# One transformer block with two token streams on one core: scale and value weights loaded in other chunks, the value products ordered by key tile, and the text's normalisation moved ahead

## The chip, the cores and the metric

The kernel runs on one core of a Trainium2 chip. The metric is the device time of one execution in microseconds; of several runs the median is given. Everything below that is called the span is the stretch from the first to the last instruction that the profiler recorded.

## What is computed

There are two streams of tokens: 2 batches of 256 image tokens and 2 batches of 32 text tokens, each token with D = 1152 features. All inputs and outputs are bf16.

```python
mod_i = (_silu(c) @ wmod_img).reshape(B, 6, 1, D)      # the same for the text: mod_t
shi, sci, gai = mod_i[:, 0], mod_i[:, 1], mod_i[:, 2]  # shift, scale, gate
hi = _layernorm(x_img) * (1 + sci) + shi
ht = _layernorm(x_txt) * (1 + sct) + sht
qkvi = hi @ wqkv_img
qkvt = ht @ wqkv_txt
...                                                    # q, k, v: text tokens first, then image tokens
p = _softmax(jnp.einsum('bqd,bkd->bqk', q, k) * D ** (-0.5))
a = jnp.einsum('bqk,bkd->bqd', p, v)
out_i = x_img + gai * (ai @ wo_img)
out_t = x_txt + gat * (at @ wo_txt)
```

Of the modulation weights only three of the six column blocks (shift, scale, gate) are read, so the weights come to 14 blocks of 1152 x 1152, 2592 KB each.

## The kernel before

The 1152 features are nine tiles of 128 ("key tiles", `kt`), the 512 image tokens four tiles of 128 (`i` = 0 to 3, two for each batch). The order of the instructions on each engine is the order of the calls in the source: nothing reorders them. All weights come through SyncE's DMA queue in the order in which `dma_start` is called, into a pool of six 2592 KB buffers (`wpool`).

The first stage prepares the image tokens and makes the values. For each token tile, VectorE takes the statistics (`stats_of`, L153), ScalarE the standard deviation (`std_of`, L160) and VectorE the normalised tile `xn_i` (`out_of`, L164 and L165). TensorE transposes the nine 128 x 128 blocks of it (`x_transposes`, L178). ScalarE copies them out of PSUM into `hT_i`: `evac_scaled` (L183) multiplies by the scale while it copies, `evac_low` (L187) and `evac_high` (L190) copy without it. The transposes go to two PSUM tiles: `n0` blocks into the first, from the seven-slot pool `ps_mm`, and the rest into a second one, from `ps_mm` for token tiles 0 and 1, from the one-slot pool `ps_sm` for tiles 2 and 3 (`n0` = 8).

The scale itself, one column for each key tile, is 9 matmuls of two columns each for a key tile (`mod_scale`, L195), whose result is evicted with 1 added (L204 or L206). Where `hT_i` was copied out before its scale was known, `apply_mod` multiplies it in place, on VectorE (L214), GpSimd (L219) or ScalarE (L223).

The image values are the products of `hT_i` with `w_v_i`: for each token tile two halves of 512 columns (and a rest of 128, `v_rest`, L340), each a sum over nine key tiles in a PSUM tile of its own (`vacc`). `v_part` issues the matmuls of one such unit for one chunk of key tiles (L235), `v_block` loops over chunks and, inside, over units. Seven of the eight units are made here and sit in `ps_mm` until their ninth matmul; the seventh unit, token tile 3's first half, gets its slot when the last transposes have been copied out. `KC` cuts both weights into chunks of key tiles, (0,2), (2,4), (4,6) and (6,9): `load_sc` loads a chunk's columns of the scale weights (rows of 256 or 384 elements, 512 or 768 bytes), `load_v` a chunk's rows of the value weights (2304 bytes each). The queue's order is x0, x1, scale 0, x2, value 0, x3, then scale and value of chunks 1, 2 and 3, then the shift weights `w_sh_i` and the query weights `w_q_i`. `warm` issues matmuls on zeros (L130): 4, 7 and, behind `mod_scale(0)`, 3.

Then come the shift of the image tokens (rows of `strip_rows`, L361 and L365, columns by `select_cols`, additions by `apply_mod`) and the query stage, `qk_img(w_q_i, 0)`: nine groups of nine matmuls of 512 columns (L450), the first three groups together, each evicted by ScalarE or VectorE in turn (L434, L436). After it TensorE makes the rows of the text's shift (`tsh`), of its scale (`tsc`) and of the values' shift term (`svr`) by `rows_for_cols` (L361, L365), evicted on VectorE, ScalarE, VectorE (`evac`, L144 and L146). Then comes the key stage, `qk_img(w_k_i, 1)`, with three hooks between its groups: before group 0 `txt_norm` normalises the text (VectorE and ScalarE, L476 to L479, with a load of ScalarE's exponential table), before group 3 `all_cols` makes the scale and shift columns, and before group 6 `txt_transposes` transposes the normalised text on TensorE (L492) and modulates it on VectorE (L494, L496). Text queries and keys (L507), scores, softmax, attention and the output products follow.

Of the kernel before, what the change touches and what calls it, by code (L numbers as in the profile page):

```python
# [8 lines left out]
ACT = mybir.ActivationFunctionType  # L9
# [5 lines left out]
def kernel(  # L15
# [21 lines left out]
    P = 128  # L37
# [8 lines left out]
    SCALE = float(D) ** -0.5  # L46
    EPS = 1e-5

    KC = [(0, 2), (2, 4), (4, 6), (6, KT)]
    VW = 512  # L50
    NM = 1024

# [36 lines left out]
    def load_x(i):  # L89
        nc.sync.dma_start(x_i[:, i, :], xi_t[:, i, :])  # L90

    def load_sc(ch):
        k0, k1 = KC[ch]
        nc.sync.dma_start(w_sc_i[:, :, k0 * P:k1 * P], w_view(wmod_img)[:, :, D + k0 * P:D + k1 * P])  # L94

    def load_v(ch):
        k0, k1 = KC[ch]
        nc.sync.dma_start(w_v_i[:, k0:k1, :], w_view(wqkv_img)[:, k0:k1, 2 * D:3 * D])  # L98

    load_x(0)  # L100
    load_x(1)
    load_sc(0)
    load_x(2)
    load_v(0)
    load_x(3)
    for ch in range(1, len(KC)):
        load_sc(ch)
        load_v(ch)
    K3 = ((0, 3), (3, 6), (6, KT))
    K2 = ((0, 5), (5, KT))  # L110
    w_sh_i = load_w(wmod_img, 0)
# [15 lines left out]
    def warm(n):  # L127
        for _ in range(n):
            ps = ps_mm.tile([P, VW], f32, tag="mm", name="wps")
            nc.tensor.matmul(ps[:], lhsT=wz[:, 0:P], rhs=wz[:], start=True, stop=True)  # L130
# [41 lines left out]
    def x_transposes(i, n0=5):  # L172
        tps = (ps_mm.tile([P, n0, P], bf, tag="mm", name="tp"),
               ps_mm.tile([P, KT - n0, P], bf, tag="mm", name="tp") if n0 == 5 else
               ps_sm.tile([P, KT - n0, P], bf, tag="sm", name="tp"))
        for kt in range(KT):
            tp = tps[0][:, kt, :] if kt < n0 else tps[1][:, kt - n0, :]
            nc.tensor.transpose(tp, xn_i[:, i, kt * P:(kt + 1) * P], ident[:])  # L178
        return tps + (n0,)

    def evac_scaled(i, tps, n):
        for kt in range(n):
            nc.scalar.activation(hT_i[:, kt, i * P:(i + 1) * P], tps[0][:, kt, :], ACT.Identity,  # L183
                                 scale=mod_i[:, KT + kt, i // TPB:i // TPB + 1])

    def evac_low(i, tps, n):
        nc.scalar.copy(hT_i[:, n:tps[2], i * P:(i + 1) * P], tps[0][:, n:tps[2], :])  # L187

    def evac_high(i, tps):
        nc.scalar.copy(hT_i[:, tps[2]:KT, i * P:(i + 1) * P], tps[1][:])  # L190
# [7 lines left out]
    def mod_scale(ch, eng, own=True):  # L198
        k0, k1 = KC[ch]
        pool, tag = (ps_sm, "sm") if own else (ps_mm, "mm")  # L200
        mps = pool.tile([P, KT, B], f32, tag=tag)
        mod_cols(w_sc_i, mps, k0, k1)
        if eng == "dve":
            nc.vector.tensor_scalar_add(mod_i[:, KT + k0:KT + k1, :], mps[:, 0:k1 - k0, :], 1.0)  # L204
        else:
            nc.scalar.activation(mod_i[:, KT + k0:KT + k1, :], mps[:, 0:k1 - k0, :], ACT.Identity, bias=1.0)  # L206

    def apply_mod(kt, t0, t1, shift, eng):
        b = t0 // TPB
        sl = hT_i[:, kt, t0 * P:t1 * P]  # L210
        ap = mod_i[:, kt, b:b + 1] if shift else mod_i[:, KT + kt, b:b + 1]
        op = ALU.add if shift else ALU.mult
        if eng == 0:
            nc.vector.tensor_scalar(sl, sl, ap, None, op0=op)  # L214
        elif eng == 1:
            if shift:
                nc.gpsimd.tensor_scalar(sl, sl, 1.0, ap, op0=ALU.mult, op1=ALU.add)
            else:
                nc.gpsimd.tensor_scalar(sl, sl, ap, 0.0, op0=ALU.mult, op1=ALU.add)  # L219
        elif shift:  # L220
            nc.scalar.activation(sl, sl, ACT.Identity, bias=ap, scale=1.0)
        else:
            nc.scalar.activation(sl, sl, ACT.Identity, scale=ap)  # L223
# [2 lines left out]

    vacc = {}

    def v_part(i, half, ch):
        k0, k1 = KC[ch]  # L230
        if ch == 0:
            vacc[i, half] = ps_mm.tile([P, VW], f32, tag="mm", name=f"va{i}{half}")
        ps = vacc[i, half]
        for kt in range(k0, k1):
            nc.tensor.matmul(ps[:], lhsT=hT_i[:, kt, i * P:(i + 1) * P], rhs=w_v_i[:, kt, half * VW:(half + 1) * VW],  # L235
                             start=(kt == 0), stop=(kt == KT - 1))
        if k1 == KT:
            evac(v_i[:, i, half * VW:(half + 1) * VW], ps[:])


    def v_block(units, chs):
        for ch in chs:
            for (i, half) in units:
                v_part(i, half, ch)

    warm(4)
    silu_c()
# [3 lines left out]
    def stats_of(i, k0, k1):  # L251
        lns[i] = ln_stats(x_i[:, i, :], P, k0, k1, lns.get(i))

    def std_of(i):
        lns[i] = ln_std(lns[i], P)

    def out_of(i):
        ln_apply(x_i[:, i, :], P, xn_i[:, i, :], *lns[i])

    stats_of(0, 0, NCH)  # L260
    std_of(0)
    stats_of(1, 0, 1)
    out_of(0)
    tps = x_transposes(0)
    stats_of(1, 1, NCH)
    evac_low(0, tps, 2)
    std_of(1)
    mod_scale(0, "act")
    evac_scaled(0, tps, 2)
    evac_high(0, tps)  # L270
    out_of(1)
    warm(3)
    tps = x_transposes(1)
    stats_of(2, 0, NCH)
    evac_scaled(1, tps, 2)
    std_of(2)
    evac_low(1, tps, 2)
    evac_high(1, tps)
    stats_of(3, 0, 1)
    out_of(2)  # L280
    v_block([(0, 0), (0, 1), (1, 0), (1, 1)], [0])
    tps = x_transposes(2, KT - 1)
    stats_of(3, 1, NCH)
    evac_scaled(2, tps, 2)
    std_of(3)
    mod_scale(1, "dve", own=False)
    for n, kt in enumerate(range(*KC[1])):
        apply_mod(kt, 0, 2, False, n)
    evac_low(2, tps, 2)
    evac_high(2, tps)  # L290
    v_block([(2, 0), (2, 1)], [0])
    out_of(3)
    for kt in range(*KC[1]):
        apply_mod(kt, 2, 3, False, 0)
    v_block([(0, 0), (0, 1)], [1])
    tps = x_transposes(3, KT - 1)
    evac_high(3, tps)
    evac_scaled(3, tps, 4)
    evac_low(3, tps, 4)
    v_block([(1, 0), (1, 1)], [1])  # L300
    mod_scale(2, "dve")
    for kt in range(*KC[2]):
        apply_mod(kt, 0, 2, False, 0)
        apply_mod(kt, 2, 4, False, 1)
    v_block([(2, 0), (2, 1)], [1])
    v_block([(3, 0)], [0, 1])
    v_i = act.tile([P, NIT, D], bf, tag="A")
    SEVEN = [(i, half) for i in range(NIT) for half in range(2)][:7]
    for (i, half) in SEVEN[:4]:
        v_part(i, half, 2)  # L310
    mod_scale(3, "dve")
    for b in range(B):
        for n, kt in enumerate(range(*KC[3])):
            apply_mod(kt, b * TPB, (b + 1) * TPB, False, (n + b) % 3)
    for (i, half) in SEVEN[4:]:
        v_part(i, half, 2)
    for (i, half) in SEVEN:
        v_part(i, half, 3)

    selF = const.tile([P, 2, 2, B, NT], bf)
    for r in range(2):
# [76 lines left out]
    evac(v_i[:, 3, VW:NM], ps[:])  # L400
    nc.gpsimd.tensor_copy(shT32[:, :, 0:B], mod_i[:, 0:KT, :])

    w_sh_t = load_w(wmod_txt, 0, K2)
    w_sc_t = load_w(wmod_txt, D, K2)
    w_k_i = load_w(wqkv_img, D, K3)
    nc.sync.dma_start(x_t[:], xt_flat[:, :])
    w_q_t = load_w(wqkv_txt, 0)
    w_k_t = load_w(wqkv_txt, D)
    w_ga_i = load_w(wmod_img, 2 * D)
# [44 lines left out]

    qk_img(w_q_i, 0, hooks={})

    tsh = rows_for_cols(w_sh_t, "tsh")
    tsc = rows_for_cols(w_sc_t, "tsc")
    svr = rows_for_cols(w_v_i, "svr", lhs=shT32)
# [10 lines left out]
    mod_t = const.tile([P, 2, KT, B], f32, name="mod_txt")  # L470
    sv_full = const.tile([P, 2 * KT + 16 + 128], f32, name="sv")
    sv = sv_full[:, 0:KT * B].rearrange("p (k b) -> p k b", b=B)
    hT_t = act.tile([P, KT, NTT], bf)
    xn_t = act.tile([NTT, D], bf)

    def txt_norm():  # L476
        ln_apply(x_t[:, :], NTT, xn_t[:, :], *ln_std(ln_stats(x_t[:, :], NTT), NTT))
        junk = small.tile([P, 1], f32, bufs=1)
        nc.scalar.activation(junk[:], eps_t[:], ACT.Exp)  # L479

    def all_cols():
        ctp = ps_sm.tile([P, 3, NCOL + B], f32, tag="sm")
# [3 lines left out]
            cols_out(mod_t[:, k, :, :], ctp[:, k, :], float(k))  # L486
        cols_out(sv, ctp[:, 2, :], 0.0)

    def txt_transposes():
        tpt = ps_mm.tile([P, KT, NTT], bf, tag="mm")  # L490
        for kt in range(KT):
            nc.tensor.transpose(tpt[:, kt, :], xn_t[:, kt * P:(kt + 1) * P], ident[0:NTT, 0:NTT])  # L492
        hv = hT_t[:].rearrange("p k (b t) -> p k b t", b=B)
        nc.vector.tensor_mul(hv, tpt[:].rearrange("p k (b t) -> p k b t", b=B),  # L494
                             mod_t[:, 1, :, :].unsqueeze(3).to_broadcast([P, KT, B, NT]))
        nc.vector.tensor_add(hv, hv, mod_t[:, 0, :, :].unsqueeze(3).to_broadcast([P, KT, B, NT]))  # L496

    qk_img(w_k_i, 1, hooks={0: txt_norm, 3: all_cols, 6: txt_transposes})

    FG = 6  # L500
    for blk, wq in enumerate([w_q_t, w_k_t]):
# [341 lines left out]
```

## Time and profile before

| what | value |
|---|---|
| time, median of three runs (lowest, highest) | 117.24 us (117.14, 117.29) |
| time of the profiled execution | 117.79 us |
| its span | 115.8 us |
| TensorE busy in the span | 110.6 us, 96% |
| VectorE, ScalarE, GpSimd busy | 53.7, 34.2, 24.0 us |
| bytes read from HBM | 39.36 MB |
| DMA rate over the span | 351 GB/s |
| 162 matmuls of the query and key stages (L450) | 35.6 us busy |
| 63 matmuls of the value units (L235) | 14.6 us busy |

The page cuts the span into 40 slices of 2.9 us. TensorE is busy for nine tenths or more of each slice from the fifth to the last but one, and the 16 DMA engines from the second to the thirty-fifth:

```profile
PE   5978999999999999999999999999999999999990
...
DMA  3999999999999999999999999999999999982052
```

Each digit is the busy share of one slice in tenths. Most of the kernel is thus limited by TensorE while the weights stream in beside it; in the first slices TensorE works on what has arrived. The profiled execution took 0.55 us more than the median of the runs; its instruction times are used below as they are, and what they sum to is laid on the median.

### The profile page before, as it was taken

The page shows a single profiled execution, that of the slowest core. Times are in us where ns is not written, and L with a number is a line of the kernel's source. Part 1 is how long each engine was busy: PE and PEld are TensorE (multiplying, and loading weights), DVE is VectorE, ACT ScalarE, POOL GpSimd, SP SyncE. Part 2 cuts the span into 40 slices and gives each one's busy share as a digit, 9 for nine tenths or more (in the row PEclk, how much of TensorE's full clock was granted, in tenths as well). Part 3 has the DMA queues.
Part 4 walks back from the last instruction along what each step waited for, and adds up shares of the span by engine and source line. Part 5 has one row for each costly group of instructions (what it writes and reads, how often), then busy time and mean ns, then how long its engine had stood idle before and what let it go on. Part 6 is the DMA issues. An engine that isn't in the chain of part 4 may idle for free.

```text
span 115.8 us, 2947 instructions
## 1 busy us (share of the span) xinstructions
PE 110.6 (96%) x1262; PEld 65.3 (56%) x1262; DVE 53.7 (46%) x138; ACT 34.2 (30%) x83; POOL 24.0 (21%) x55
## 2 busy tenths in 40 slices
PE   5978999999999999999999999999999999999990
PEld 1344563548644444486444445987677665568570
DVE  1689920354290312211572332136665804994771
ACT  4548660343270320121080121116455700000200
POOL 4000103660050000002215000000240300999000
PEclk9999999999999999999999999999999999999999
DMA  3999999999999999999999999999999999982052
GB/s 83 297 338 359 376 385 399 409 412 415 404 408 408 413 412 400 414 410 294 375 404 411 396 376 381 404 412 402 412 408 405 404 416 410 409 297 108 6 187 68
DMA packets 22840, 40.89 MB, mean 353 GB/s; under 512 B 1183, under 2 KB 6699, under 8 KB 22827
## 3 DMA queue, kind: packets, MB, share of 16 engines
q1 hardware_dynamic: 22032, 39.82, 91.8%
q0 software_dynamic: 480, 0.73, 1.7%
q8 instruction: 10, 0.16, 0.5%
q10 hardware_dynamic: 315, 0.14, 0.5%
q14 instruction: 3, 0.02, 0.1%
HBM read 39.36 MB, written 1.34 MB: 351 GB/s over the span
## 4 chain that ended last, share of the span: by engine, by line
PE 80%; SPq 9%; DMA 8%; issue 1%; DVE 1%
PE qkps L450 30%; PE ps L762 15%; DMA w_sc_i<-in_wmod_img_dram 8%; PE va L235 5%; SPq L98 5%; PE aps L671 5%; PE ps L507 4%; PE sps L531 4%; PE gps L361 4%; SPq L90 3%; PE ops L783 2%; PE ps L395 2%; PE ps L340 2%; PE ps L603 2%; SPq L94 1%; PE gps L423 1%
## 5 line engine op out<-in xcount | busy, mean ns | idle before, releaser
L450 PE MATMUL qkps<-hT_i,t 128*128 128x512 bf16 x162 | 35.6, 379 | 0.0
L450 PEld LDWEIGHTS <-t 128*128 128x128 bf16 x162 | 15.6, 98 | 18.6
L762 PE MATMUL ps<-t,aT 128*128 128x384 bf16 x99 | 16.4, 326 | 0.0
L762 PEld LDWEIGHTS <-aT 128*128 128x128 bf16 x117 | 11.1, 98 | 6.7 <-issue 0.2
L235 PE MATMUL va<-w_v_i,hT_i 128*128 128x512 bf16 x63 | 14.6, 379 | 0.2 <-ACT hT_i L183 0.2
L746 POOL TENSOR_TENSOR w_og<-t,gb 128x384 bf16<-128x384 bf16 x9 | 8.7, 996 | 6.1 <-DMA gb<-mod_scratch 6.1
L235 PEld LDWEIGHTS <-hT_i 128*128 128x128 bf16 x63 | 5.8, 97 | 6.8 <-ACT hT_i L190 0.3
L768 DVE TENSOR_TENSOR tmp<-ps,gb 128x384 bf16<-128x384 f32 x11 | 6.0, 549 | 4.9 <-DMA gb<-mod_scratch 4.2
L434 DVE TENSOR_SCALAR qkT<-qkps 128x512 bf16<-128x512 f32 x4 | 2.8, 692 | 11.4 <-PE qkps L450 11.4
L153 DVE BATCH_NORM_STATS2 stats<-x_i 128x6 f32<-128x384 bf16 x12 | 6.0, 542 | 2.6 <-DMA x_i<-in_x_img_dram 2.6
L130 PE MATMUL wps<-wz 128*128 128x512 bf16 x14 | 5.9, 574 | 1.2 <-DVE wz L120 1.2
L436 ACT ACTIVATE qkT<-qkps 128x512 bf16<-128x512 f32 x5 | 2.9, 596 | 13.6 <-PE qkps L450 13.6
L144 DVE CAST qkT<-qkps 128x512 bf16<-128x512 f32 x4 | 2.8, 692 | 6.7 <-PE qkps L450 6.7
L219 POOL TENSOR_SCALAR hT_i<-hT_i,mod_img 128x256 bf16<-128x256 bf16 x5 | 2.5, 510 | 16.1 <-ACT rstd L160 9.6
L146 ACT CAST qkT<-qkps 128x512 bf16<-128x512 f32 x5 | 2.8, 582 | 9.7 <-PE qkps L450 9.7
L558 POOL DMA_DIRECT2D mod_scratch<-g_sb x2 | 1.2, 583 | 20.7 <-ACT g_sb L556 20.7
L769 DVE TENSOR_TENSOR o<-tmp,x_i 128x384 bf16<-128x384 bf16 x11 | 5.2, 471 | 0.4
L684 DVE TENSOR_SCALAR aT<-aps,sv 128x288 bf16<-128x288 f32 (+2 forms) x11 | 4.3, 456 | 2.3 <-PE aps L671 2.3
L507 PEld LDWEIGHTS <-t 128*128 128x128 bf16 x162 | 4.9, 98 | 0.2
L507 PE MATMUL ps<-hT_t,t 128*128 128x64 bf16 x162 | 4.9, 193 | 0.0
L738 ACT CAST gbf_full<-bps 128x288 bf16<-128x288 f32 x2 | 0.7, 402 | 14.2 <-PE bps L736 14.2
L671 PE MATMUL aps<-pT,v_i 128*128 128x288 bf16 (+2 forms) x44 | 4.8, 264 | 0.1
(156 smaller groups left out, 139.8 us busy)
## 6 DMA issues: line engine op xcount, KB each, us to landing
t<-in_wmod_img_dram SPq DMA_DIRECT2D x2, 2592.0 KB, 19.3
t<-in_wqkv_img_dram SPq DMA_DIRECT2D x6, 864.0 KB, 13.8
t<-in_wqkv_txt_dram SPq DMA_DIRECT2D x2, 2592.0 KB, 18.4
t<-in_wmod_txt_dram SPq DMA_DIRECT2D x2, 1440.0 KB, 15.0
t<-in_wqkv_txt_dram SPq DMA_DIRECT2D x3, 864.0 KB, 16.0
t<-in_wmod_txt_dram SPq DMA_DIRECT2D x1, 2592.0 KB, 19.5
t<-in_wo_txt_dram SPq DMA_DIRECT2D x3, 864.0 KB, 15.3
t<-in_wmod_txt_dram SPq DMA_DIRECT2D x2, 1152.0 KB, 16.2
```

Source lines behind the costliest of these rows:

```text
L98: nc.sync.dma_start(w_v_i[:, k0:k1, :], w_view(wqkv_img)[:, k0:k1, 2 * D:3 * D])
L130: nc.tensor.matmul(ps[:], lhsT=wz[:, 0:P], rhs=wz[:], start=True, stop=True)
L153: nc.vector.bn_stats(stats[0:np_, k, :], x_ap[:, k * CH:(k + 1) * CH])
L235: nc.tensor.matmul(ps[:], lhsT=hT_i[:, kt, i * P:(i + 1) * P], rhs=w_v_i[:, kt, half * VW:(half + 1) * VW], start=(kt == 0), stop=(kt == K ...
L361: nc.tensor.matmul(gps[32 * g:32 * g + 32, 0:RC], lhsT=lhs[:, kt, :], rhs=wt[:, kt, g * RC:(g + 1) * RC], start=(kt == 0), stop=(kt == KT ...
L450: nc.tensor.matmul(pss[j - j0][:], lhsT=wq[:, kt, j * P:(j + 1) * P], rhs=hT_i[:, kt, :], start=(kt == 0), stop=(kt == KT - 1))
L507: nc.tensor.matmul(ps[:, j - j0, :], lhsT=wq[:, kt, j * P:(j + 1) * P], rhs=hT_t[:, kt, :], start=(kt == 0), stop=(kt == KT - 1))
L671: nc.tensor.matmul(bank[:, off:off + c1 - c0], lhsT=lhsT, rhs=rhs, start=(first[id(bank)] == n), stop=(final[id(bank)] == n))
L746: nc.gpsimd.tensor_mul(w_og[:, dt, 0:CH], w_o_i[:, dt, NG0:D], gb[:, B - 1, NG0:D])
L762: nc.tensor.matmul(ps[:, 0:cw], lhsT=aT[:, dt, t0:t0 + P], rhs=rhs, start=(dt == DTS[0]), stop=(dt == DTS[-1]))
L768: nc.vector.tensor_mul(tmp[:, 0:cw], ps[:, 0:cw], gb[:, b, cs])
L769: nc.vector.tensor_add(o[:, cs], tmp[:, 0:cw], x_i[:, i, cs])
```

## The change

`KC` has three chunks of three key tiles in place of four. The scale weights come in three DMAs of 864 KB with rows of 768 bytes; the value weights come in single key tiles (288 KB) and pairs (576 KB): the queue's order is x0, x1, scale 0, x2, v0, v1, x3, v2, scale 1, v3, v4-5, scale 2, v6, v7-8. `v_k` replaces `v_part` and `v_block`: for each key tile, in the outer loop, one matmul of each unit. The order of the calls in the first stage is written anew around it. `warm(2)` stands ahead of `mod_scale(0)` in place of `warm(3)` behind it; `evac_high(0)` stands ahead of it too. The text's weights `w_sh_t` and `w_sc_t` are one DMA each and `x_t` is loaded ahead of `w_k_i`. The text is normalised behind the query stage, ahead of the rows `tsh`; it is transposed behind the rows `svr` and copied to `hT_t` by ScalarE, and VectorE modulates it in place at the key stage's group 6.

```diff
-    KC = [(0, 2), (2, 4), (4, 6), (6, KT)]
+    KC = [(0, 3), (3, 6), (6, KT)]
...
-    def load_v(ch):
-        k0, k1 = KC[ch]
+    def load_v(k0, k1):
         nc.sync.dma_start(w_v_i[:, k0:k1, :], w_view(wqkv_img)[:, k0:k1, 2 * D:3 * D])
...
     load_sc(0)
     load_x(2)
-    load_v(0)
+    load_v(0, 1)
+    load_v(1, 2)
     load_x(3)
+    load_v(2, 3)
     for ch in range(1, len(KC)):
+        k0, k1 = KC[ch]
         load_sc(ch)
-        load_v(ch)
+        load_v(k0, k0 + 1)
+        load_v(k0 + 1, k1)
...
-    def evac_scaled(i, tps, n):
-        for kt in range(n):
+    def evac_scaled(i, tps, n, n0=0):
+        for kt in range(n0, n):
...
-    def v_part(i, half, ch):
...
-    def v_block(units, chs):
...
+    def v_k(units, *kts):
+        for kt in kts:
             for (i, half) in units:
-                v_part(i, half, ch)
+                if kt == 0:
+                    vacc[i, half] = ps_mm.tile([P, VW], f32, tag="mm", name=f"va{i}{half}")
+                ps = vacc[i, half]
+                nc.tensor.matmul(ps[:], lhsT=hT_i[:, kt, i * P:(i + 1) * P], rhs=w_v_i[:, kt, half * VW:(half + 1) * VW],
+                                 start=(kt == 0), stop=(kt == KT - 1))
+                if kt == KT - 1:
+                    evac(v_i[:, i, half * VW:(half + 1) * VW], ps[:])
...
+    U = [[(i, half) for half in range(2)] for i in range(NIT - 1)] + [[(NIT - 1, 0)]]
+    U01, U012, UALL = U[0] + U[1], U[0] + U[1] + U[2], U[0] + U[1] + U[2] + U[3]
...
     tps = x_transposes(0)
+    evac_low(0, tps, 3)
+    warm(2)
     stats_of(1, 1, NCH)
-    evac_low(0, tps, 2)
     std_of(1)
+    evac_high(0, tps)
     mod_scale(0, "act")
-    evac_scaled(0, tps, 2)
-    evac_high(0, tps)
+    evac_scaled(0, tps, 3)
     out_of(1)
-    warm(3)
     tps = x_transposes(1)
     stats_of(2, 0, NCH)
     evac_scaled(1, tps, 2)
     std_of(2)
-    evac_low(1, tps, 2)
+    evac_scaled(1, tps, 3, 2)
+    evac_low(1, tps, 3)
     evac_high(1, tps)
-    stats_of(3, 0, 1)
     out_of(2)
-    v_block([(0, 0), (0, 1), (1, 0), (1, 1)], [0])
+    v_k(U01, 0, 1)
     tps = x_transposes(2, KT - 1)
-    stats_of(3, 1, NCH)
-    evac_scaled(2, tps, 2)
+    stats_of(3, 0, NCH)
+    evac_scaled(2, tps, 3)
     std_of(3)
-    mod_scale(1, "dve", own=False)
-    for n, kt in enumerate(range(*KC[1])):
-        apply_mod(kt, 0, 2, False, n)
-    evac_low(2, tps, 2)
+    evac_low(2, tps, 3)
     evac_high(2, tps)
-    v_block([(2, 0), (2, 1)], [0])
     out_of(3)
+    v_k(U01, 2)
+    v_k(U[2], 0, 1, 2)
+    mod_scale(1, "dve")
     for kt in range(*KC[1]):
-        apply_mod(kt, 2, 3, False, 0)
-    v_block([(0, 0), (0, 1)], [1])
+        apply_mod(kt, 0, 2, False, 0)
+        apply_mod(kt, 2, 3, False, 1)
     tps = x_transposes(3, KT - 1)
+    evac_scaled(3, tps, 3)
+    evac_low(3, tps, 3)
     evac_high(3, tps)
-    evac_scaled(3, tps, 4)
-    evac_low(3, tps, 4)
-    v_block([(1, 0), (1, 1)], [1])
+    for kt in range(*KC[1]):
+        apply_mod(kt, 3, 4, False, 0)
+    v_k(U012, 3)
+    v_k(U[3], 0, 1, 2)
+    v_i = act.tile([P, NIT, D], bf, tag="A")
+    v_k(U012, 4)
+    v_k(U[3], 3, 4)
     mod_scale(2, "dve")
...
+    v_k(UALL, *range(5, KT))
...
-    w_sh_t = load_w(wmod_txt, 0, K2)
-    w_sc_t = load_w(wmod_txt, D, K2)
+    w_sh_t = load_w(wmod_txt, 0)
+    w_sc_t = load_w(wmod_txt, D)
+    nc.sync.dma_start(x_t[:], xt_flat[:, :])
     w_k_i = load_w(wqkv_img, D, K3)
-    nc.sync.dma_start(x_t[:], xt_flat[:, :])
...
     qk_img(w_q_i, 0, hooks={})
 
+    hT_t = act.tile([P, KT, NTT], bf)
+    xn_t = act.tile([NTT, D], bf)
+    ln_apply(x_t[:, :], NTT, xn_t[:, :], *ln_std(ln_stats(x_t[:, :], NTT), NTT))
+    junk = small.tile([P, 1], f32, bufs=1)
+    nc.scalar.activation(junk[:], eps_t[:], ACT.Exp)
     tsh = rows_for_cols(w_sh_t, "tsh")
     tsc = rows_for_cols(w_sc_t, "tsc")
     svr = rows_for_cols(w_v_i, "svr", lhs=shT32)
...
+    tpt = ps_mm.tile([P, KT, NTT], bf, tag="mm")
+    for kt in range(KT):
+        nc.tensor.transpose(tpt[:, kt, :], xn_t[:, kt * P:(kt + 1) * P], ident[0:NTT, 0:NTT])
+    nc.scalar.copy(hT_t[:], tpt[:])
...
-    def txt_transposes():
...
+    def txt_mod():
         hv = hT_t[:].rearrange("p k (b t) -> p k b t", b=B)
-        nc.vector.tensor_mul(hv, tpt[:].rearrange("p k (b t) -> p k b t", b=B),
-                             mod_t[:, 1, :, :].unsqueeze(3).to_broadcast([P, KT, B, NT]))
+        nc.vector.tensor_mul(hv, hv, mod_t[:, 1, :, :].unsqueeze(3).to_broadcast([P, KT, B, NT]))
         nc.vector.tensor_add(hv, hv, mod_t[:, 0, :, :].unsqueeze(3).to_broadcast([P, KT, B, NT]))
 
-    qk_img(w_k_i, 1, hooks={0: txt_norm, 3: all_cols, 6: txt_transposes})
+    qk_img(w_k_i, 1, hooks={3: all_cols, 6: txt_mod})
```

More of the change, by code (lines that the diff above doesn't have):

```diff
@@ L227 @@
     vacc = {}
-    def v_part(i, half, ch):
[L230 to L238, printed above, removed]
-    def v_block(units, chs):
-        for ch in chs:
-            for (i, half) in units:
-                v_part(i, half, ch)
+    def v_k(units, *kts):
+        for kt in kts:
+            for (i, half) in units:
+                if kt == 0:
[5 more added lines that the diff above has]
+                    evac(v_i[:, i, half * VW:(half + 1) * VW], ps[:])
     warm(4)
@@ L276 @@
     std_of(2)
-    evac_low(1, tps, 2)
+    evac_scaled(1, tps, 3, 2)
+    evac_low(1, tps, 3)
     evac_high(1, tps)
-    stats_of(3, 0, 1)
     out_of(2)
-    v_block([(0, 0), (0, 1), (1, 0), (1, 1)], [0])
+    v_k(U01, 0, 1)
     tps = x_transposes(2, KT - 1)
-    stats_of(3, 1, NCH)
-    evac_scaled(2, tps, 2)
+    stats_of(3, 0, NCH)
+    evac_scaled(2, tps, 3)
     std_of(3)
-    mod_scale(1, "dve", own=False)
-    for n, kt in enumerate(range(*KC[1])):
-        apply_mod(kt, 0, 2, False, n)
-    evac_low(2, tps, 2)
+    evac_low(2, tps, 3)
     evac_high(2, tps)
-    v_block([(2, 0), (2, 1)], [0])
     out_of(3)
+    v_k(U01, 2)
+    v_k(U[2], 0, 1, 2)
+    mod_scale(1, "dve")
     for kt in range(*KC[1]):
-        apply_mod(kt, 2, 3, False, 0)
-    v_block([(0, 0), (0, 1)], [1])
+        apply_mod(kt, 0, 2, False, 0)
+        apply_mod(kt, 2, 3, False, 1)
     tps = x_transposes(3, KT - 1)
+    evac_scaled(3, tps, 3)
+    evac_low(3, tps, 3)
     evac_high(3, tps)
-    evac_scaled(3, tps, 4)
-    evac_low(3, tps, 4)
-    v_block([(1, 0), (1, 1)], [1])
-    mod_scale(2, "dve")
[L302 to L311, printed above, removed]
+    for kt in range(*KC[1]):
[5 more added lines that the diff above has]
+    v_k(U[3], 3, 4)
+    mod_scale(2, "dve")
     for b in range(B):
-        for n, kt in enumerate(range(*KC[3])):
+        for n, kt in enumerate(range(*KC[2])):
             apply_mod(kt, b * TPB, (b + 1) * TPB, False, (n + b) % 3)
[L315 to L318, printed above, removed]
+    v_k(UALL, *range(5, KT))
     selF = const.tile([P, 2, 2, B, NT], bf)
@@ L472 @@
     sv = sv_full[:, 0:KT * B].rearrange("p (k b) -> p k b", b=B)
[L473 to L479, printed above, removed]
+    tpt = ps_mm.tile([P, KT, NTT], bf, tag="mm")
+    for kt in range(KT):
+        nc.tensor.transpose(tpt[:, kt, :], xn_t[:, kt * P:(kt + 1) * P], ident[0:NTT, 0:NTT])
+    nc.scalar.copy(hT_t[:], tpt[:])
     def all_cols():
@@ L487, in all_cols @@
         cols_out(sv, ctp[:, 2, :], 0.0)
-    def txt_transposes():
-        tpt = ps_mm.tile([P, KT, NTT], bf, tag="mm")
-        for kt in range(KT):
-            nc.tensor.transpose(tpt[:, kt, :], xn_t[:, kt * P:(kt + 1) * P], ident[0:NTT, 0:NTT])
+    def txt_mod():
         hv = hT_t[:].rearrange("p k (b t) -> p k b t", b=B)
-        nc.vector.tensor_mul(hv, tpt[:].rearrange("p k (b t) -> p k b t", b=B),
-                             mod_t[:, 1, :, :].unsqueeze(3).to_broadcast([P, KT, B, NT]))
+        nc.vector.tensor_mul(hv, hv, mod_t[:, 1, :, :].unsqueeze(3).to_broadcast([P, KT, B, NT]))
         nc.vector.tensor_add(hv, hv, mod_t[:, 0, :, :].unsqueeze(3).to_broadcast([P, KT, B, NT]))
-    qk_img(w_k_i, 1, hooks={0: txt_norm, 3: all_cols, 6: txt_transposes})
+    qk_img(w_k_i, 1, hooks={3: all_cols, 6: txt_mod})
     FG = 6
```

## The prediction

> **What bounds the kernel now.** I read the chain of waits first, in order of time (start, length, what; microseconds):
>
> ```profile
> 11.42 8.79 DMA w_sc_i<-in_wmod_img_dram
> 20.21 0.05 issue
> 20.26 0.83 PE mps L195 x27
> 21.09 6.00 PE va L235 x27
> 27.09 2.01 PE ps L340 x36
> ```
>
> The last scale chunk, issued at 11.42, lands at 20.21; from there TensorE (PE) carries the chain to 113.06 but for 0.38 us near 85.6. Second, all that PE waited for in the whole span (total, times, longest):
>
> ```profile
> PE wps L130 <- DVE wz L120: 1.2, 1, 1.2
> PE tp L178 <- DVE xn_i L165: 0.6, 2, 0.4
> PE mps L195 <- DMA w_sc_i<-in_wmod_img_dram: 0.2, 1, 0.2
> PE va L235 <- ACT hT_i L183: 0.2, 1, 0.2
> ```
>
> All lie in the first 10 us. So past 27 us the change can only add waits, and what it can win is PE's gaps before that. Third, PE's timeline around 20 us:
>
> ```profile
> 16.58 3.61 PE L235 MATMUL va<-w_v_i,hT_i 128*128 128x512 bf16 x16
> 20.26 0.83 PE L195 MATMUL mps<-sT,w_sc_i 128*128 128x2 bf16 x27
> 20.95 6.14 PE L235 MATMUL va<-w_v_i,hT_i 128*128 128x512 bf16 x27
> 26.92 1.28 PE L340 MATMUL ps<-w_v_i,hT_i 128*128 128x128 bf16 x20
> ```
>
> Prices: a value matmul is issued every (3.61-0.38)/15 = 0.216 us (0.38: one matmul's mean); 27 scale matmuls hold PE 20.95-20.26 = 0.69; nine transposes 0.52 (11.90 to 12.41). The first block of 16 is issued by 20.04, so **PE arrives only 0.2 us ahead of the scale chunk**: two chains end together here, and shortening one alone brings little. The last 27 matmuls take 26.92-20.95 = 5.97, 0.15 more than 27 x 0.2155 = 5.82: PE waited for the last value chunk, landed at 22.35.
>
> **The loads.** Ahead of the last scale chunk stand 5472 KB as before. What changes is that 1728 KB of scale weights come as 2304 packets of 768 bytes, not 3456 of 512. The trace's packets last 27 and 36 ns: (3456 x 27 - 2304 x 36)/16 = 0.65 us saved. By landings (576 KB in 12.20-10.53 = 1.67 us, 23.2 ns a packet on each engine; the last chunk, less one instruction fetch of 0.96 us among its packets, in 20.21-16.81-0.96 = 2.44 us, 33.9 ns) it is 216 x 23.2 - 144 x 33.9 = 0.13 us. Rates (window, length, four busy times, clock, DMA share, GB/s) speak for the lesser:
>
> ```profile
> 13.00:14.00 1.00, 1.00 (x6) 0.38 (x5) 0.85 (x5) 1.00 (x4) 0.54 (x1) 1.00 1.14 352
> 16.00:16.50 0.50, 0.50 (x17) 0.38 (x16) 0.00 (x0) 0.50 (x3) 0.00 (x0) 1.00 1.05 364
> 20.00:22.00 2.00, 1.94 (x33) 1.18 (x33) 0.84 (x3) 0.61 (x2) 0.62 (x2) 1.00 1.04 410
> ```
>
> These are rows of mostly 512, 768 and 2304 bytes. I take 0.15: the last scale chunk lands at 20.06, PE may use it at 20.11. The value rows in smaller DMAs cost nothing: image tile x3, 288 KB, landed 0.72 us behind the DMA ahead of it (10.53, 9.81), 410 GB/s; SyncE's extra issue (0.43) lies under the queue it has filled.
>
> [...]
>
> **The first scale chunk** is 288 KB larger, the step with the least cover. It landed at 7.63 with 72 packets an engine. Bounds: the same packets, same time, 7.63; or, as its 3.17 us behind x1 (4.46) grow with bytes, 9.2. I take 72 x (33.9-23.2) = +0.77: 8.40. x2 goes from 8.34 to 9.11.
>
> **PE's order from there**, ScalarE (ACT) first, by these rows (start, length):
>
> ```profile
> 12.56 0.62 ACT L183 ACTIVATE hT_i<-tp,mod_img 128x128 bf16<-128x128 bf16 x2 [0.67 <-PE tp L178]
> 13.08 0.29 ACT L160 ACTIVATE rstd<-mv,eps_t 128x1 f32<-128x1 f32 x1
> 13.28 0.78 ACT L187 COPY hT_i<-tp 128x768 bf16<-128x768 bf16 x1
> 13.96 0.27 ACT L190 COPY hT_i<-tp 128x128 bf16<-128x128 bf16 x1
> ```
>
> A scaled block takes 0.26 (result 0.31 after its start), a deviation 0.2, a copy of five blocks about 0.6, of one 0.16; ACT starts 0.66 after the first transpose.
> - Scale 0: PE 8.45 to 9.14; ACT's addition at 9.32 (0.87 after PE, as L204 at 21.12), scaled blocks from 9.52. Transposes 1 from 9.14 (before: 9.10): the lost `warm(3)` costs nothing, PE would wait anyway.
> - Statistics of tile 2 start with x2 at 9.16 (8.96), so `xn_i` 2 is ready at 12.04 (11.84) and its transposes start at 12.09 (11.90). The eight value matmuls before them end at 11.95. The later x2 costs 0.19.
> - Value matmuls k2 of tiles 0 and 1 and k0-2 of tile 2: ten, 12.61 to 14.77. ACT: three scaled blocks from 12.75, deviation 3 at 13.77, copies to 14.84. `mod_scale(1)` now takes the one-slot pool, where transposes 2's last block lies, and waits for that copy: 14.89 to 15.58. Queued behind it on PE are transposes 3, whose input is ready at 14.87: 0.12 lost.
> - Transposes 3 to 16.10, k3 of six units from 16.27 (VectorE's first scaling) to 17.57. The seventh unit needs the slot that ACT empties at 17.77: 0.2 lost; its three end at 18.42, six k4 at 19.71, two at 20.15.
>
> So PE reaches the last scale chunk at **20.15**, the DMA 20.11: against 20.26, -0.11. Behind it stand 27 scale matmuls as before and 28 value matmuls, not 27: +0.216. k5 fills 1.5 us, so the value wait of 0.15 goes: the last rows are landed by 22.2, and k7 is due at 23.9. The seven evictions now come at 0.216 us, not 0.65, and take 0.69 on VectorE: the first ends 1.11 us behind its matmul's issue (0.42 lag, as 23.24 behind 22.82), while `v_rest`, which takes its slot, comes 1.51 behind. Hidden by 0.4. Sum: -0.11 + 0.22 - 0.15 = **-0.04 us**.
>
> **The text.** Nine transposes (0.37 us at 65.50) move to 53.44 and cost the same there; ACT's copy and VectorE's modulation lie under 18 us of key matmuls. The waits are new: VectorE, ahead of evicting `tsh` and `svr`, and ACT, ahead of `tsc`, stand behind `x_t`.
>
> ```profile
> 48.05 0.69 DVE L434 TENSOR_SCALAR qkT<-qkps 128x512 bf16<-128x512 f32 x1 [3.19 <-PE qkps L450]
> 56.41 1.47 DVE L153 BATCH_NORM_STATS2 stats<-x_t 64x6 f32<-64x384 bf16 x3 [2.30 <-DMA x_t<-in_x_txt_dram]
> 53.44 2.76 PE L450 MATMUL qkps<-hT_i,t 128*128 128x512 bf16 x12
> ```
>
> `x_t` came at 56.4, behind `w_k_i`; it now comes behind `w_sc_t`, landed at 48.15, plus 0.4. VectorE is free at 48.74; statistics and deviation to 50.9, normalised by 51.7 (57.91-56.41 and 0.57, with ACT's last query copy, 49.99 to 50.59, ahead of the deviation). PE asks at 53.44: 1.7 us cover, without which each us late is a us of PE. `w_k_i` comes 0.36 later; its last third landed at 55.68 and is due at 53.44 + 18 x 0.216 = 57.3. Nothing on the path.
>
> The profiled 117.79 (span 115.8 and 2.0 around it) becomes 117.75; laid on the median of 117.24, **117.2**.
>
> **Rivals.**
> - *ACT's waits are shorter than worked out* (faster). Slot, one-slot pool and k3's scaling cost 0.2 + 0.12 + 0.17 by pitches from other shapes. Without them PE arrives at 19.66; it gains only if the DMA gain is 0.65 (19.61), which also brings the shift weights, landed at 28.74 and due at 29.02, in time: -0.04 - 0.49 = -0.5, 116.7. For: packet durations; against: the landings. 0.24.
> - *The first scale chunk comes later* (slower). Deviation 2 and everything behind hang on it and on x2, one us for one us past 8.4; the kernel is over 0.2% slower (0.23 us, about what a measurement here can tell from no change) from 8.68 on. At 9.2: +0.76, 118.0. For: 44 ns a packet in that stretch; against: a first packet of 1.36 us in it, which does not grow with rows. 0.20.
> - *`x_t` late, or PE's clock falls.* The first pays past 50.3, 118 at 51.1. The warm-ups ran at 0.43 us each until 6.3, the eight matmuls at 9.95 at 0.216. A warm-up less and an idle PE from 7.9 to 8.45 could bring eight slow ones, +1.7, 118.9. 0.09 together. [...]
> - *The change does not hasten the loads.* Chunk at 20.21, PE at 20.26: +0.07, 117.3. 0.08.
>
> **Numbers.** The forecast has 0.39, own range 117.0 to 117.4, of which 0.06 lies beyond -0.2%. Faster 0.24 + 0.06 = 0.30; same 0.33 + 0.08 = 0.41; slower 0.29. The range takes in the first rival's price and half of the second's, and leaves out the latest of the slow cases: 116.6 to 117.8.
>
> **What would show it.** Scale 0's matmuls near 8.45, transposes 2 near 12.1, the last scale matmuls near 20.15 with PE just busy before them, `v_rest` near 26.88, no PE wait at the text's transposes near 53.4. Wrong if the last scale matmuls start before 19.8 or after 20.5, if `v_rest` waits for an eviction, or if the slots' waits are missing.

## The result and the profile after

| | before | after |
|---|---|---|
| time, median (lowest, highest) of 6 runs each | 117.41 us (117.14, 117.85) | 118.83 us (118.11, 119.90) |
| time and span of the profiled execution | 117.79, 115.8 | 118.11, 116.1 |
| ratio, with its 95% interval | | 1.0107 [1.0066, 1.0148] |

The changed kernel is slower by 1.4 us, outside the range of 116.6 to 117.8. The profiled execution of it is the fastest of the six runs and the only one whose TensorE clock stayed at full speed; in the other five the recorded mean clock is 0.984 or 0.985, and their median is 118.98. The ratio leaves out disturbed runs, the latest of those with a fallen clock among them, here and in the table of the experiments, so that it understates a kernel whose clock falls often. Two things have to be found: what costs time at full clock, and why the clock falls.

At full clock, first the chain of waits of the changed kernel (start, length, what):

```profile
1.65 7.36 DMA w_sc_i<-in_wmod_img_dram
9.06 0.84 PE mps L198 x27
...
10.13 1.15 ACT hT_i L186 x4
...
20.86 0.66 PE mps L198 x27
21.52 1.75 PE va L238 x8
23.32 4.26 PE va L238 x19
27.58 2.01 PE ps L330 x36
...
53.79 0.22 PE gps L355 x8
54.01 0.37 PE tpt L470 x9
```

Before, the chain's DMA was the last scale chunk (to 20.21). Now it is the first, to 9.01, and TensorE carries the chain from there, with short pieces of ScalarE and VectorE in between. The text's transposes (54.01) follow the row before them without a gap, as forecast.

TensorE's waits in the same execution (total, times, longest):

```profile
PE mps L198 <- DMA w_sc_i<-in_wmod_img_dram: 1.3, 1, 1.3
PE wps L133 <- DVE wz L123: 1.2, 1, 1.2
PE tp L181 <- DVE xn_i L168: 0.9, 1, 0.9
PE va L238 <- ACT hT_i L186: 0.2, 1, 0.2
```

The wait for the first chunk was 0.2 us and is 1.3. TensorE's timeline (start, length; the idle time before it in brackets) gives the starts that the prediction named:

```profile
9.06 0.83 PE L198 MATMUL mps<-sT,w_sc_i 128*128 128x2 bf16 x27 [1.31 <-DMA w_sc_i<-in_wmod_img_dram]
...
12.76 0.68 PE L181 MATMUL tp<-ident,xn_i 128*128 128x128 bf16 x9
...
20.70 0.82 PE L198 MATMUL mps<-sT,w_sc_i 128*128 128x2 bf16 x27
21.38 6.20 PE L238 MATMUL va<-w_v_i,hT_i 128*128 128x512 bf16 x27
27.42 0.78 PE L330 MATMUL ps<-w_v_i,hT_i 128*128 128x128 bf16 x11
```

| step | before | forecast | after |
|---|---|---|---|
| first scale products | 7.68 | 8.45 | 9.06 |
| transposes of tile 2 | 11.90 | 12.09 | 12.76 |
| second scale products | 12.41 | 14.89 | 15.49 |
| last scale chunk lands (DMA records) | 20.21 | 20.06 | 19.59 |
| last scale products | 20.26 | 20.15 | 20.70 |
| `v_rest` | 26.92 | 26.88 | 27.42 |

The step from the first to the last scale products was forecast at 11.70 and took 11.64; from there to `v_rest` 6.73 and 6.72. Every row of TensorE is late against the forecast by about what the first one is late, 0.54 to 0.67 us; the last scale chunk is early by 0.47. The last scale products at 20.70 lie past 20.5, which the prediction had named as a sign that it is wrong. Against the kernel before, `v_rest` is late by 0.50; at the start of the last matmul 0.32 of that is left (113.14 against 112.83), and the span ends 2.96 us behind that start in both.

### The profile page after: what moved, and what is told of

The parts are those of the page before. It is cut to its first block, busy times and chain, and to the rows that moved or that the text cites. A ratio compares the mean times of both kernels' runs of the same rounds, so it can differ in the third digit from the quotient of the medians.

```text
span 116.1 us, 2940 instructions
## 1 busy us (share of the span) xinstructions
PE 109.1 (94%) x1254; PEld 65.1 (56%) x1261; DVE 53.6 (46%) x138; ACT 35.0 (30%) x86; POOL 23.8 (21%) x55
## 4 chain that ended last, share of the span: by engine, by line
PE 87%; DMA 6%; ACT 1%; DVE 1%; issue 1%; SPq 1%
PE qkps L440 30%; PE ps L750 15%; PE va L238 12%; DMA w_sc_i<-in_wmod_img_dram 6%; PE aps L659 5%; PE ps L495 4%; PE sps L519 4%; PE gps L351 4%; PE mps L198 2%; PE ops L771 2%; PE ps L385 2%; PE ps L330 2%; PE ps L591 2%; PE gps L413 1%; PE sps L532 1%; ACT hT_i L186 1%
## 5 line engine op out<-in xcount | busy, mean ns | idle before, releaser
L133 PE MATMUL wps<-wz 128*128 128x512 bf16 x13 | 5.1, 538 | 1.2 <-DVE wz L123 1.2
L222 POOL TENSOR_SCALAR hT_i<-hT_i,mod_img 128x128 bf16<-128x128 bf16 (+1 forms) x5 | 2.2, 454 | 16.8 <-DVE mod_img L207 16.8
L217 DVE TENSOR_SCALAR hT_i<-hT_i,mod_img 128x256 bf16<-128x256 bf16 (+1 forms) x17 | 4.4, 320 | 1.1 <-ACT hT_i L190 1.0
```

## The experiments

All runs, in microseconds. "Full" are runs with a recorded clock of 0.99 or more, "fallen" those below (0.968 to 0.986). "Over before" compares full runs with full runs of the kernel before on the same chip (medians 117.31 for e1 to e4, 117.37 for e5 to e8, 117.46 for e9 to e12, 117.34 for e13 to e15; of its 113 runs there 6 had fallen).

| run | median | full: runs, median, over before | fallen: runs, median | ratio [95%] |
|---|---|---|---|---|
| e13 changed kernel again | 118.77 | 3, 117.66, +0.32 | 9, 119.33 | 1.0053 [1.0018, 1.0089] |
| e1 first stage alone | 118.04 | 7, 117.78, +0.47 | 5, 119.49 | 1.0051 [1.0024, 1.0078] |
| e2 text alone | 117.55 | 11, 117.53, +0.22 | 1, 118.20 | 1.0022 [1.0004, 1.0041] |
| e3 changed, 8 warm-ups | 117.99 | 10, 118.00, +0.69 | 0 | 1.0060 [1.0040, 1.0080] |
| e4 before, no `warm(3)` | 118.25 | 4, 117.34, +0.03 | 8, 118.41 | 1.0051 [1.0023, 1.0079] |
| e5 before, first chunk of three | 119.50 | 2, 117.79, +0.42 | 9, 120.02 | 1.0105 [1.0065, 1.0146] |
| e6 before, text loads | 117.60 | 12, 117.60, +0.23 | 0 | 1.0019 [1.0002, 1.0035] |
| e7 text without its loads' new cut | 117.31 | 11, 117.27, -0.10 | 1, 118.12 | 0.9995 [0.9974, 1.0016] |
| e8 changed, chunks 2, 4, 3 | 118.79 | 6, 118.79, +1.42 | 0 | 1.0106 [1.0084, 1.0129] |
| e9 before, six more DMAs | 117.47 | 11, 117.42, -0.04 | 1, 118.62 | 0.9996 [0.9969, 1.0023] |
| e10 before, x2 ahead | 118.22 | 6, 117.52, +0.06 | 6, 119.28 | 1.0028 [0.9994, 1.0061] |
| e11 e3 with two DMAs more | 118.25 | 6, 118.25, +0.79 | 0 | 1.0063 [1.0040, 1.0086] |
| e12 text and last value chunk | 117.89 | 12, 117.89, +0.43 | 0 | 1.0026 [1.0001, 1.0051] |
| e14 changed, x2 ahead, 8 warm-ups | 118.85 | 6, 118.84, +1.50 | 0 | 1.0140 [1.0103, 1.0178] |
| e15 before, x2 ahead, 4 more warm-ups | 117.50 | 12, 117.50, +0.16 | 0 | 1.0011 [0.9989, 1.0033] |

### The halves (e1, e2) and the clock (e3, e4)

e1 has the changed first stage with the old text, e2 the old first stage with the changed text. e3 and e4 touch nothing but warm-up matmuls on zeros:

```diff
 e3 (changed kernel)      e4 (kernel before)
-    warm(2)             -    warm(3)
+    warm(8)
```

> The changed kernel's first stage with the text part of before. The profiled execution of the changed kernel lost 0.5 us by 27 us and 0.3 us at its end, the median of its runs lost 1.4 us, and in five of its six runs the mean granted clock was 0.985 (1.000 in the profiled one). Theory A (the first stage alone is the loss: the scale weights' first chunk lands later, 9.01 against 7.63, and the longer idle time of TensorE ahead of it lets its clock fall): 1.2 to 1.6 us over before, most runs at a clock near 0.985. Theory B (what goes beyond the profiled 0.3 us comes from the text part): 0.3 us over before, clock near 1.000.

> Before with the text part of the change alone. Theory A: within 0.2 us of before, clock near 1.000. Theory B: about 1 us over before.

> The changed kernel with eight warm-up matmuls, not two, ahead of the first scale product: at 0.216 us each they fill TensorE from 7.15 to about 8.9, where it stood idle from 7.74 to 9.06. Theory A: the granted clock is 1.000 again in nearly all runs, and the time is 0.3 us over before (the later chunk is still there). Theory B, or a fall of the clock elsewhere: no change against the changed kernel, 1.2 to 1.6 us over before.

> Before without the three warm-up matmuls behind the first scale product, nothing else changed: 0.65 us less of full-width work on TensorE between 8.1 and 9.0 us. If the number of warm-up matmuls by itself decides over the clock: a mean granted clock near 0.985 in part of the runs and up to 1 us over before. If it takes the long idle stretch ahead of the later chunk: clock 1.000, within 0.2 us of before.

At full clock the halves come to 0.47 + 0.22 = 0.69, and e3 has 0.69 in ten runs that all kept the clock. That they agree is luck. The trace of e1 has 0.36 us of its loss behind the last matmul, in an end that the changed kernel does not have (last section), and its `v_rest` starts at 26.65, earlier than before, because its first chunk landed at 8.27. In e3 the chunk landed at 8.01, and what the products waited for were the eight warm-ups:

```profile
7.27 1.89 PE L133 MATMUL wps<-wz 128*128 128x512 bf16 x8
8.99 0.82 PE L198 MATMUL mps<-sT,w_sc_i 128*128 128x2 bf16 x27
```

The changed kernel itself has +0.32 in e13, from three runs that spread from 117.25 to 118.25, and one run at 118.11 in the result.

e4 makes the clock's fall appear in the kernel before, by three matmuls less: full runs cost nothing (+0.03), fallen ones +1.07, and two thirds of the runs fall. So the fall does not need the chunk, and it is neither the chip's nor the text's; in these runs it goes with how much TensorE does in the first stage (three matmuls fewer than before in e4: 8 falls in 12 runs; six more than the changed kernel in e3: none in ten). The page of e13, the changed kernel again, shows it in the clock's row (40 slices of 2.9 us):

```profile
PEclk9996799999999999999999999999999999999999
```

In windows cut at the clock's records (columns: window; its length; busy time and instructions of PE, weight load, VectorE, ScalarE, GpSimd; clock; DMA share; GB/s), e13:

```profile
6.30:9.70 3.40, 2.10 (x44) 1.58 (x44) 2.43 (x7) 1.24 (x4) 0.00 (x0) 1.00 1.04 370
9.70:13.10 3.40, 3.18 (x14) 1.33 (x12) 2.97 (x8) 2.77 (x10) 0.00 (x0) 0.50 1.07 383
13.10:16.50 3.40, 3.40 (x39) 2.02 (x38) 1.65 (x5) 1.81 (x6) 0.00 (x0) 1.00 1.06 391
```

and e4:

```profile
6.60:10.00 3.40, 2.21 (x37) 1.72 (x39) 2.97 (x9) 2.37 (x8) 0.00 (x0) 1.00 1.03 383
10.00:13.40 3.40, 3.21 (x13) 1.50 (x13) 2.91 (x8) 1.34 (x4) 0.00 (x0) 0.50 1.10 374
```

In e2, e5, e13 and e4 a window of 3.40 us has the clock at 0.50 (8.20 to 11.60, 9.30 to 12.70, 9.70 to 13.10 and 10.00 to 13.40), and the windows beside it stand at 1.00 (in e5 the one ahead). The mean clock of these executions is 0.985, in e4 0.982. e10's is 0.971 over 118.9 us, by which 2 x 0.029 x 118.9 = 6.9 us would be at half speed, twice as much. In e13's slow stretch 14 matmuls ran, though TensorE was busy for 3.18 of 3.40 us. The fall puts e13's `v_rest` 19.26 us behind the first scale products, 0.9 to 1.1 more than in the full-clock traces of the same stage (18.17 to 18.36).

The window ahead of the stretch was not idle: TensorE was busy for 2.10 and 2.21 us. Many of those matmuls have two columns, though. Counted in columns, with a full window at 2.4 a nanosecond (a 512-column matmul every 0.216 us, rounded), the 3.4 us ahead of the fall held 37% of a full window in e13, 35% in e4, 40% in e2's one fallen run, 15% in e5, 27% in e10. Where the clock stayed, windows of the same length, counted from the first record at full speed, held 47% (before, 3876 columns), 39 and 40% (the profiled run of the changed kernel, 3200 and 3254), 45 and 46% (e1), 52 and 65% (e3). So in these traces falls came behind 15 to 40% and the clock stayed behind 39 to 65%; the 47% of the kernel before are 7 points above the fullest window that a fall followed. The two ranges meet: a window of 3236 columns (40%) came before the fall in e2 and kept the clock in e8.

At half clock, e10's first slow window had 32% and a second one followed, while full speed came back behind windows with 42% (e13) to 52% (e5). Busy time does not sort these windows (1.35 to 2.20 us ahead of a fall, but 1.83 in the profiled run of the changed kernel, which kept the clock), nor does the longest idle time in them (0.96 to 1.53 us ahead of a fall, 1.29 in e11, which kept it).

When the clock first opens differs from run to run, 4.4 to 6.9 us in the traces, so that the windows lie differently. That this is why the same kernel falls in some runs only is argued from that, and not shown.

### Which edit costs at full clock (e5, e6, e7, e9)

e5 is the kernel before with a first scale chunk of three key tiles and a second of one. e6 is the kernel before with the text's loads as changed; e7 the kernel before with the text's instructions moved and `x_t` ahead of `w_k_i`, but the weights in two DMAs each; e9 adds two DMAs to each of three later weights.

```diff
 e5, in load_sc
-        k0, k1 = KC[ch]
+        k0, k1 = [(0, 3), (3, 4), (4, 6), (6, KT)][ch]
 e6
-    w_sh_t = load_w(wmod_txt, 0, K2)
-    w_sc_t = load_w(wmod_txt, D, K2)
+    w_sh_t = load_w(wmod_txt, 0)
+    w_sc_t = load_w(wmod_txt, D)
+    nc.sync.dma_start(x_t[:], xt_flat[:, :])
     w_k_i = load_w(wqkv_img, D, K3)
-    nc.sync.dma_start(x_t[:], xt_flat[:, :])
 e9, the same for w_k_t and w_ga_i
-    w_q_t = load_w(wqkv_txt, 0)
+    w_q_t = load_w(wqkv_txt, 0, K3)
```

> Before, with the scale weights' first DMA taking three key tiles and the second one (the products still in chunks of 2, 2, 2 and 3). If the later first chunk is what the 0.47 us at full clock of the first stage alone are: its products start near 9.0 us, not 7.68, the rest of the first stage stands 0.4 to 0.6 us later at 27 us, and the time at full clock is 0.4 to 0.6 us over before; TensorE then also waits longer ahead of the products, so that the clock falls in part of the runs though the three warm-up matmuls behind them are still there. If the order of the first stage's instructions (products by key tile, the slots, the one-slot pool) is what costs: at most 0.2 us over before.

> Before with the text's loads of the change alone (scale and shift weights in one DMA each, x_t ahead of the image keys' weights). The text part alone took 0.22 us more than before at the same span of 115.4 us, so its loss lies outside the span. If it is these loads: 0.2 us over before with a span of 115.4; if it is the moved instructions: the same time as before.

> Before with the text part of the change, but with its scale and shift weights in two DMAs each as in before (two DMAs more than in the text part alone). If the number and size of these DMAs makes the 0.22 us outside the span: the same time as before. If the moved instructions make it: 0.2 us over before.

> Before, with three of its 2592 KB loads (the text's queries, the text's keys, the image's gate) in three DMAs each: six DMAs more. The time outside the span was 1.92 us in before, 1.80 in the two kernels with one DMA more, 2.11 and 2.18 in the two with two DMAs less. Theory (about 0.1 us outside the span for each DMA that a kernel has less): 1.3 us outside, 0.6 us under before. Rival (what counts are the DMAs of the text's scale and shift weights, or their place): 1.9 outside and no change.

e5 alone brings +0.42 at full clock (two runs only), with the same stretch from the last matmul to the end as before (2.95 us), and nine falls in eleven runs. TensorE's timeline of e5:

```profile
8.86 0.60 PE L195 MATMUL mps<-sT,w_sc_i 128*128 128x2 bf16 x18 [1.53 <-DMA w_sc_i<-in_wmod_img_dram]
9.32 1.44 PE L130 MATMUL wps<-wz 128*128 128x512 bf16 x3
```

It waits 1.53 us for the larger chunk, and the three warm-ups behind it then run at 0.43 us each, at half clock. Over the traces of these runs a first chunk of three key tiles landed at 8.01 to 9.13 us (six traces, those with x2 ahead of it left out, median 8.75), one of two at 7.16 to 7.92 (eight, median 7.39): +1.36. In e5 x2 comes later too, at 9.57 against 8.34, so that its +0.42 need not be the chunk's products alone.

In the kernel before, the text's 0.22 is its loads': e6 has all of it, e7 none. It lies for the most part outside the span. The medians of the span are 115.4 (before) and 115.5 (e6), of the time outside it 1.92 and 2.10; e7 has 1.94. The guess that each DMA less costs 0.1 us there fell with e9: six DMAs more, -0.04. In the changed kernel the loss is not to be seen: outside its span lie 1.85 us in e13's full runs, as in the kernel before on that chip, and 2.00 against 1.92 in e3.

### Attempts at a better order (e8, e10, e11, e12, e14, e15)

```diff
 e8 (chunks of the changed kernel; text as before; order of the first stage fitted)
-    KC = [(0, 3), (3, 6), (6, KT)]
+    KC = [(0, 2), (2, 6), (6, KT)]
 e10 and e15 (before), e14 (changed)
-    load_sc(0)
     load_x(2)
+    load_sc(0)
```

e14 and e15 add warm-ups as well (`warm(8)` for `warm(2)`; four more behind the first transposes). e11 is e3 with the text's weights in two DMAs each; e12 is the changed text on the old first stage, with those loads as before, the last value chunk in two DMAs and by key tiles, and e9's six DMAs.

> The changed kernel's products by key tile and value rows in single tiles, but the scale weights in chunks of 2, 4 and 3 key tiles, the warm-up matmuls and the text as in before. Theory (first chunk and clock are the whole loss, the order by key tile costs nothing): the first product starts near 7.7, the clock is 1.000 as in before, TensorE ends the seven value units at 26.5 to 26.9 us, against 26.92, and the time is 0 to 0.4 us under before. Rival (the order by key tile itself costs): 0.2 us and more over before.

> Before, with the third image tile issued ahead of the first scale chunk: the tile lands at about 7 us, not 8.34, the chunk at about 8.35, not 7.63. If the chunk's own products carry the delay: TensorE's work at 27 us stands 0.4 us or more later and the time at full clock is 0.3 to 0.5 us over before. If the delay of the changed kernel came through the third tile's statistics, which its larger first chunk also holds up: no loss here, within 0.1 us of before.

> The changed kernel with eight warm-up matmuls ahead of the first scale product and its text's scale and shift weights in two DMAs each: two of the three losses undone. If they add up: full clock in all runs, 117.8 us, 0.4 to 0.5 us over before, all of it the later first chunk. If the three overlap: 0.2 us from that on either side.

> Before with the moved text (its weights in two DMAs each), the last value rows in a single tile and a pair with their 21 products by key tile, and three loads in three DMAs each. The first chunk and the warm-ups are those of before, so the clock stays as in before. If by key tile the wait of 0.15 us for the last value rows goes, the moved text gives 0.1 us, and the DMAs 0.7 us: 116.4 to 116.7 us. If the DMAs give nothing: 117.1, about 0.2 under before.

> The changed kernel with eight warm-up matmuls ahead of the first scale product (so that the clock stays, 118.00 us in the earlier run) and the third image tile issued ahead of the first scale chunk. The tile lands at about 6, not 9.8 us, the chunk 0.7 us later than it did. If the third tile's statistics carry the loss of the first stage: 0.3 to 0.5 us less than with the eight warm-ups alone. If the chunk's products carry it: 0.4 to 0.7 us more.

> Before with the third image tile ahead of the first scale chunk and four warm-up matmuls ahead of the first scale product, which fill the wait for the later chunk. Without these the clock fell in six of twelve runs, and at full clock the time was 0.06 us over before. If a clock that falls is the missing work in that wait: no falls now. If the chunk's products carry the delay in before's order of instructions: 0.3 to 0.5 us over before; if the tile's statistics do: within 0.15 us of before.

e8 was a miss. With the small first chunk all six runs kept the clock, but TensorE came late to the last scale products, by waits between 11 and 15 us that the fitted order made, and 0.42 of its 1.42 lies behind the last matmul (last section). Its timeline:

```profile
12.95 1.04 PE L237 MATMUL va<-w_v_i,hT_i 128*128 128x512 bf16 x4 [0.41 <-ACT hT_i L185]
14.25 1.04 PE L197 MATMUL mps<-sT,w_sc_i 128*128 128x2 bf16 x36 [0.26 <-ACT hT_i L192]
...
21.71 0.82 PE L197 MATMUL mps<-sT,w_sc_i 128*128 128x2 bf16 x27
```

e10, e14 and e15 delay the first chunk by the 288 KB of x2 and bring x2 forward. They tell whether the changed kernel hangs on the chunk or on x2. TensorE's timeline of e14:

```profile
10.16 0.83 PE L198 MATMUL mps<-sT,w_sc_i 128*128 128x2 bf16 x27 [0.90 <-DMA w_sc_i<-in_wmod_img_dram]
...
21.62 0.82 PE L198 MATMUL mps<-sT,w_sc_i 128*128 128x2 bf16 x27
```

and of e15:

```profile
8.68 0.60 PE L195 MATMUL mps<-sT,w_sc_i 128*128 128x2 bf16 x18 [0.33 <-DMA w_sc_i<-in_wmod_img_dram]
...
20.33 0.82 PE L195 MATMUL mps<-sT,w_sc_i 128*128 128x2 bf16 x27
```

In the changed kernel 1.17 us more on the chunk's products (10.16 against 8.99 in e3) reach the last scale products whole (21.62 against 20.44) and cost 0.84 us of the time (118.84 against 118.00), though x2 landed at 7.15: the start of the chunk's products carries. The traces say the same without an experiment: in the five full-clock ones with the changed first stage (the changed kernel, e1, e3, e11, e14) `v_rest` starts 18.17 to 18.36 us behind the first scale products, which start anywhere from 8.32 to 10.16. In the kernel before, 1.00 us more (8.68 against 7.68) end in 0.07 (20.33 against 20.26), since TensorE there runs into the last scale chunk: in the traces of before, e6, e7 and e9 `v_rest` starts 6.70 to 6.73 us behind that chunk's landing (19.73 to 20.22). And between e10 and e15 four warm-ups took the falls from six runs of twelve to none.

e11 and e12 were misses too. Two DMAs each for the text's weights should have won e3's 0.2 us back. Outside the span they did (1.78 against 2.00), but the end behind the last matmul grew by 0.36 (3.32 against 2.96), and e11 stands at +0.79. e12 was to beat the kernel before and is 0.43 slower: in its profile `v_rest` starts 0.15 us earlier than before (26.77), and the end is 0.59 longer (last section). None of these kernels is shown to be faster than the one before; e7 and e9 equal it.

## Why the prediction was wrong

Two steps failed: the first scale chunk, by its size, and the lost `warm(3)`, which was put at nothing.

**The first scale chunk.** Costed by the packets' pitch of a later stretch, +0.77, it came 1.38 later between the two profiles (9.01 against 7.63) and 1.36 in the medians of all traces. The bound "as its 3.17 us behind x1 grow with bytes, 9.2", +1.59, was named and not taken, and is the nearer. The argument against it, that a first packet's 1.36 us in that stretch does not grow, would have left (3.17 - 1.36)/2 = 0.9 for the added 288 KB; it does not fit. The second rival, with its point of 8.68, happened: 9.01 is 0.33 past that point. Nearly one for one, as the rival put it, the 0.61 us went through transposes 2 and both later scale products to `v_rest` (0.54). So the stage's end hangs on the first chunk where it hung on the last one, and against the forecast of -0.04 the changed kernel measured +0.32 at full clock (e13, three runs).

**The DMA's gain was mis-sized the other way, and could not be used.** The last scale chunk came 0.62 us earlier (19.59), near the 0.65 of the packets' durations, not 0.15. Between the medians of seven traces with the old cut (20.09; one of them at 18.90) and five with the new (19.48) it is 0.61. That the rows' width alone did it was argued from the packets and not tried. TensorE came 1.1 us behind it (20.70), so that nothing of it was gained. The first rival's faster case needed both chains early.

**The text: no wait, but its loads cost.** Statistics started at 49.73, the normalised tile was done by 52.6, the transposes ran at 53.94 with no wait, and the moved instructions cost nothing (e7: -0.10 at full clock, interval of the ratio on both sides of 1). The cut of the text's loads, costed at nothing, costs 0.2 us in the kernel before, mostly outside the span (e6), though not visibly in the changed one. The prediction had no term for time outside the span, or for the end behind the last matmul: it took both as fixed.

**The clock is the larger part, and was held for unlikely.** That "the lost `warm(3)` costs nothing, PE would wait anyway" holds for TensorE's time alone; e4 takes out these three matmuls and nothing else, and the clock falls in 8 runs of 12. "A warm-up less and an idle PE" was named, and priced at +1.7; the third rival had 0.09 with `x_t` in it. It happened in 14 of the changed kernel's 18 runs, at +1.67 in e13 (119.33 against 117.66, three full runs) and +1.71 in e1 (119.49 against 117.78). The trace of before misled: its clock at 1.00 throughout does not tell that the first window at that clock held 47% of full work, where e2's clock fell behind 40%. The later chunk adds to the lost warm-up: TensorE does nothing for 1.3 us ahead of it, and e5, which has the later chunk and keeps the three warm-ups, fell in nine runs of eleven. At full clock the changed kernel took 117.66 in e13 and 118.11 in one run of the result, with a fallen clock 119.33 and 118.98 in the middle: the fall is the larger part both times. Its price spreads, 1.07 in e4 and up to 1.71 in e1, more than one slow window cost in e13's trace; what the rest is stays open but for the runs with two such windows.

Right were the two ends on one path (the gain in loading does not show in the time), the waits between the first chunk and `v_rest`, and the cover of `v_rest`'s eviction: TensorE has no wait there.

## What to carry to other kernels

The DMA at the head of the queue was costed better here by its bytes at the rate of its own stretch (1.59 for a measured 1.36) than by the pitch of packets later on (0.77); and a small first chunk that lets the next engine start (first scale products at 7.68, not 9.06) was worth more here than rows with which the last chunk landed 0.62 us earlier. Before warm-up matmuls are taken away, count the columns that TensorE streams in each 3.4 us: here the clock went to 0.50 for 3.4 us behind windows with 15 to 40% of full work and stayed behind windows with 39 to 65%, a cost that a single profile at clock 1.00 does not show. The end behind the last matmul and the time outside the span belong into the sum when the number or the cut of DMAs changes.

## What the runs showed of the chip that was not expected

The clock fell to 0.50 behind windows of 3.40 us in which TensorE was busy for 2.21 us (e4) and 2.10 us (e13).

The stretch behind the last matmul went with the DMA semaphore that the last output uses. In the traces SyncE's last instructions wait for eight DMA semaphores one after the other, 0.06 to 0.09 us between the starts of the first six in the traces of before and after. In the kernel before and in the changed one, the last output's is the last of the eight, and the span ends 2.96 us behind the start of the last matmul. In e6 two more waits follow the last output's, and the stretch is 3.07; in e1 and e11 six, and it is 3.32; in e8 seven, and it is 3.38. Up to 0.4 us (3.38 against 2.96) thus went with how the DMAs fall on the semaphores. That this decides it was seen in the records, one trace for each kernel, and not tried by an experiment of its own. e12's stretch of 3.55 is not of this kind: one wait follows, and behind the eight 0.5 us more pass than before, for which the trace shows no reason.

The time outside the span, in medians of full-clock runs, ranges from 1.78 (e11) to 2.18 us (e2). It is not the number of DMAs alone (e9), nor the cut of the text's loads alone (2.18 in e2 and 2.10 in e6, but 1.85 in e13); what makes it differ stays open.
